# One convolution filter's rows, transposed on VectorE inside partition quadrants and loaded in four parts

## The chip, the core and the metric

The kernel runs on one core of one Trainium2 chip. The metric is the device time of one execution, in microseconds (us). Engines are named as the profile names them: PE (TensorE's matmuls), PEld (its weight loads), DVE (VectorE), ACT (ScalarE), POOL (GpSimd) and SP (SyncE, whose queue issues most of the DMAs). L278 is line 278 of the kernel before.

## What is computed

All inputs are bf16. `x` is [2048, 512] (tokens by channels); the filter `ssm_k` is [512, 2048] (channels by taps), so it takes 2 MB.

```python
kv = shift(k) * v            # shift: four taps per channel, along the tokens
y  = irfft(rfft(kv_padded) * rfft(ssm_k_padded))[:2048]   # a causal convolution per channel, 2048 long
y  = y + kv * ssm_D          # one factor per channel
h  = x + layernorm(x) * y
out = h + relu(layernorm(h) @ w1) @ w2      # w1 [512, 1376], w2 [1376, 512]
```

## The kernel before

The convolution is done in the frequency domain, with a Fourier transform cut into two stages of small matmuls; all tables of sines are made on the chip. The order of the work on each engine is written out by hand (`tc.manual_schedule()`), so each engine executes its instructions in the order in which the code issues them. Four PSUM buffers of two banks each (`bank2`) go round in turn.

**The front of the kernel**, which the change is about, makes two things: the filter's first-stage spectrum, and `kv`.

- *Loads* (L123 to L137, all on SP's queue). The four shift taps; then `ssm_k` in one DMA of 2 MB (L124), where partition p gets the four channels p, 128+p, 256+p and 384+p, a row of 4 KB each; then eight transposing DMAs: of `k` and `v` in four pieces of 512 tokens each (k0, v0, k1, v1, ... here), which put channels on partitions and tokens along the row. `ssm_D` comes over ACT's queue.
- *Fills* (L158): 22 matmuls on zeros, whose result nobody reads.
- *Tables.* POOL makes index ramps and two unit matrices (L162 to L184), a mask `dmask` that carries `ssm_D` in 16 copies (L236) and products of indices (L238). DVE makes the first-stage matrices `f1hi` and `f1lo` (L210 to L215), the product `tsn` (L222) and reductions of it and of `r2` (`wrap13`, L220). ACT takes the sines (L147, L226, L262) and makes the 16 diagonal matrices of the shift taps (L204).
- *The filter's rows* (`to_rows`, L271 to L284, called at L312). Two bf16 values make one 32-bit word. 32 PE transposes of 128 by 128 words put time groups on the partitions and channels along the row; ACT and DVE copy them from PSUM to `kfl` (L281, L283).
- *Stage one* (`stage1`, L286 to L309): for each group `gb` of 0 to 7, 32 small matmuls (L294), then two sums with `dmask` on DVE (L306) and two casts on ACT (L309). Groups 0 and 1 read channels 0 to 31 of each row of `kfl`, 2 and 3 the next 32, and so on.
- *Taps* (`taps`, L329 to L337): for each piece c and half h, eight matmuls with the diagonals give the shifted `k` in PSUM, and DVE multiplies it by `v` in place (L337). This needs k's piece c on PE, v's on DVE.

The loop at L343 goes through groups 0 to 6, with one `taps` behind each of the first six, and sines and index work between; `taps(3, 0)` and `taps(3, 1)` stand ahead of group 6. Behind the loop POOL makes tables (L360 to L385), the transposes of `kv` (L391, `to_rows` again) wait for the last product of the taps, group 7 follows, and the rest of the kernel (spectrum of `kv`, products, inverse transform, the two layer norms and the two matmuls with `w1` and `w2`) follows in PE's order. The results leave in 17 stores (L679) on ACT's queue. Their target's address pattern is 4 blocks of 32 rows:

```python
dst = bass.AP(tensor=out_d.tensor, offset=out_d.offset + t * D + d0, ap=[[16 * D, 4], [64 * D, 32], [1, w]])
nc.scalar.dma_start(out=dst, in_=o[:, d0:d0 + w])
```

Of the kernel before, what the change touches and what calls it, by code (L numbers as in the profile page):

```python
# [9 lines left out]
ALU = mybir.AluOpType  # L10
BF16 = mybir.dt.bfloat16
F32 = mybir.dt.float32
# [3 lines left out]
P = 128  # L16
# [40 lines left out]
def kernel(  # L57
# [13 lines left out]
    nc = tc.nc  # L71
# [5 lines left out]
    DC = D // P  # L77
# [13 lines left out]
    early = pl.push("early", side="right")  # L91
# [5 lines left out]
    BK = bkp.tile([P, 2, 32, 32, DC * 2], F32R, tag="K", name="BK")  # L97
# [21 lines left out]
    r2 = G[:, 0:2048].rearrange("p (a b) -> p a b", a=32)  # L119
# [1 line left out]

    wsh = consts.tile([P, DC, KS], BF16, name="wsh")
    nc.sync.dma_start(out=wsh[:], in_=A_shift_k.rearrange("(r p) j -> p r j", p=P))  # L123
    nc.sync.dma_start(out=sk, in_=A_ssm_k.rearrange("(c p) t -> p c t", p=P))  # L124
    draw = small([DC * P], BF16)
    for dp in range(2):
        src = bass.AP(tensor=A_ssm_D.tensor, offset=A_ssm_D.offset, ap=[[0, 1], [1, DC * P]])
# [1 line left out]
    zero = consts.tile([P, P], BF16, name="zero")  # L129
    nc.vector.memset(zero[:], 0.0)  # L130
    nc.vector.memset(kT[0][:, :, 0:16], 0.0)
    for c in range(4):
        if c == 0:
            nc.sync.dma_start_transpose(out=kT[c][:, :, 16:CH + 16], in_=k_d[0:CH, :])
        else:
            nc.sync.dma_start_transpose(out=kT[c], in_=k_d[CH * c - 16:CH * c + CH, :])
        nc.sync.dma_start_transpose(out=vT[:, :, CH * c:CH * c + CH], in_=v_d[CH * c:CH * c + CH, :])  # L137

    TURN = 2.0 * math.pi * SIN_SHRINK
    nbias = consts.tile([P, 1], F32, name="nbias")  # L140
# [16 lines left out]

    fill(bank2("psz")[:, 0, :], 22)  # L158

    n1i = early.tile([P, 1], I32, name="n1i")  # L160
    for s in range(0, P, 32):
# [6 lines left out]
    r3 = small([64], I32)  # L168
# [4 lines left out]
        nc.gpsimd.memset(f[:], 0.0)  # L173
    ident = early.tile([P, P], BF16, name="ident")
    identw = early.tile([P, P], F32, name="identw")
    for t in (identw, ident):
        nc.gpsimd.memset(t[:], 0.0)
        nc.gpsimd.affine_select(out=t[:], in_=t[:], compare_op=ALU.not_equal, fill=1.0,
                                base=0, pattern=[[-1, P]], channel_multiplier=1)
    nc.gpsimd.iota(r2, pattern=[[2, 32], [128, 64]], base=1, channel_multiplier=0)  # L180
    pi4 = consts.tile([P, 2], I32, name="pi4")
    nc.gpsimd.iota(pi4[:], pattern=[[0, 2]], base=0, channel_multiplier=1)
# [10 lines left out]
    _turns(nc, t1[:, 0:32], r1[:], n1c[:], 128, True)  # L193
    _turns(nc, t1[:, 32:64], r1[:], n1c[:], 128, False)
    t3 = small([2, 64], I32)
    _turns(nc, t3[:, 0, :], r3[:], n2c[:], 64, True)
    _turns(nc, t3[:, 1, :], r3[:], n2c[:], 64, False)
    f1f = small([64], F32)
    f1d = small([64], F32)
    _sin(f1f[:, 0:32], t1[:, 0:32], 128)  # L200
    _sin(f1f[:, 32:64], t1[:, 32:64], 128, neg=True)
    for rg in range(DC):
        for j in range(KS):
            nc.scalar.mul(out=wdiag[:, rg, j, :], in_=ident[:], mul=wf[:, rg, j:j + 1])  # L204
    dsc = small([2, 64], F32)
    dpm = small([2, 64], F32)
    _sin(dsc[:], t3[:], 64)

    f1h = small([64], BF16)
    nc.vector.tensor_copy(out=f1h, in_=f1f)  # L210
# [7 lines left out]
    def wrap13(t):  # L218

        nc.vector.tensor_scalar(out=t, in0=t, scalar1=19, scalar2=19, op0=ALU.logical_shift_left, op1=ALU.arith_shift_right)  # L220

    nc.vector.tensor_single_scalar(out=tsn, in_=r2, scalar=n2c[:], op=ALU.mult)  # L222
    wrap13(tsn)

    def big_sin(out, turns, scale):
        nc.scalar.activation(out=out, in_=turns, func=ACT.Sin, scale=scale * TURN / 8192)  # L226

    dmask = early.tile([P, 2, 2, 16, 2, DC], BF16, name="dmask")
    nc.gpsimd.memset(dmask[:], 0.0)
    for dp in range(2):  # L230
        row = slice(64 * dp, 64 * dp + 1)
        for rp in range(2):
            for sp in range(2):
                src = draw[row, 256 * rp:256 * rp + 256].rearrange("p (r u s l d) -> p r u s l d", r=2, s=2, l=2, d=2)[:, :, :, sp, :, dp]
                for w in range(2):
                    nc.gpsimd.tensor_copy(out=dmask[row, rp, sp, :, w].rearrange("p u (r l) -> p r u l", l=2), in_=src)  # L236

    nc.gpsimd.tensor_scalar(out=r2, in0=r2, scalar1=n2c[:], scalar2=2048.0, op0=ALU.mult, op1=ALU.add)  # L238

# [9 lines left out]
    def ec_turns(q):  # L249
        w = ecw[q]  # L250
        nc.gpsimd.iota(w[:, 1, :].rearrange("p (i a n) -> p i a n", i=4, a=4), pattern=[[1, 4], [16, 4], [64, 32]],
                       base=4 * q, channel_multiplier=0)
        for h, off in ((0, 4096 + 2048), (1, 0)):
            nc.gpsimd.tensor_scalar(out=w[:, h, :], in0=w[:, 1, :], scalar1=k1o[:], scalar2=float(off),
                                    op0=ALU.mult, op1=ALU.add)

    def ec_wrap(q):
        nc.vector.tensor_single_scalar(out=ecw[q], in_=ecw[q], scalar=8191, op=ALU.bitwise_and)
# [12 lines left out]
    def to_rows(src, h, fl):  # L271

        srcw = src.bitcast(F32).rearrange("p c (a w) -> p (c a) w", w=32)
        o = fl.bitcast(I32)
        for eng, i0, n in {1: (("D", 0, 8),), 3: (("A", 0, 4), ("D", 4, 4))}.get(h, (("A", 0, 8),)):
            pst = bank2("pst").rearrange("p b (i c) -> p (b i) c", i=4)[:, 0:n]
            for i in range(n):
                nc.tensor.transpose(out=pst[:, i, :], in_=srcw[:, :, 8 * h + i0 + i], identity=identw[:])  # L278
            oi = o[:, :, 8 * h + i0:8 * h + i0 + n]
            if eng == "A":  # L280
                nc.scalar.copy(out=oi.bitcast(F32), in_=pst.rearrange("p i c -> p c i"))  # L281
            else:
                nc.vector.tensor_single_scalar(out=oi, in_=pst.bitcast(I32).rearrange("p i c -> p c i"),  # L283
                                               scalar=0, op=ALU.bitwise_or)  # L284
# [23 lines left out]
                                    .to_broadcast([P, 8, 16, 4]), op=ALU.add)  # L308
            nc.scalar.copy(out=o[1 - rp][:, 1], in_=pv[1 - rp][:, 1])  # L309

    for h in range(4):
        to_rows(sk, h, kfl)  # L312
    wrap13(r2)
    for t, sh, op in ((0, 2, ALU.logical_shift_right), (1, 3, ALU.bitwise_and)):
        nc.vector.tensor_single_scalar(out=pi4[:, t:t + 1], in_=pi4[:, t:t + 1], scalar=sh, op=op)
    nc.vector.tensor_scalar(out=k1o[:], in0=pi4[:, 0:1], scalar1=2.0, scalar2=1.0, op0=ALU.mult, op1=ALU.add)
    nc.vector.tensor_copy(out=rof[:], in_=pi4[:, 1:2])
    for t, v in ((esc, TURN / 8192), (ebi, -0.5 * TURN)):
        nc.vector.tensor_scalar(out=t[:], in0=rows4[:], scalar1=rof[:], scalar2=v, op0=ALU.is_equal, op1=ALU.mult)
    big_sin(st[:, :, 0:64], tsn, 1)  # L320

    def more_sines(i):
        half = slice(16 * (i % 2), 16 * (i % 2) + 16)
        if i < 2:
            big_sin(st[:, half, 128:192], tsn[:, half], -1)
        else:
            big_sin(st[:, half, 64:128], r2[:, half], 1)

    def taps(c, h, each=2):  # L329
        ps = bank2("pkv")  # L330
        for i in range(2):
            for j in range(KS):
                nc.tensor.matmul(out=ps[:, i, :], lhsT=wdiag[:, 2 * h + i, j, :],  # L333
                                 rhs=kT[c][:, 2 * h + i, 16 - j:CH + 16 - j], start=(j == 0), stop=(j == KS - 1))
# [5 lines left out]
    inv3 = consts.tile([P, 2, 2, 64], F32R, name="inv3")  # L340
    inv12 = consts.tile([P, 2, 64], F32R, name="inv12")
    ones = consts.tile([P, P], F32R, name="ones")
    for gb in range(7):  # L343
        if gb == 6:
            taps(3, 0)
            taps(3, 1, 1)
            ec_sins(0, (2, 3))
        stage1(kfl, BK, gb, dmask)
        if gb < 4:
            more_sines(gb)  # L350
        if gb == 1:
            ec_turns(0)
        if gb == 3:
            ec_wrap(0)
        if gb in (4, 5):
            ec_sins(0, (gb - 4,))
        if gb < 6:
            taps(gb // 2, gb % 2)

    nc.gpsimd.memset(inv3[:].bitcast(F32), 0.0)  # L360
    nc.gpsimd.tensor_tensor(out=dpm[:, 0, :], in0=dsc[:, 0, :], in1=dsc[:, 1, :], op=ALU.add)
# [396 lines left out]
```

## Time and profile before

| | |
|---|---|
| median of 3 runs | 210.63 us (210.59 to 212.22) |
| the profiled execution's own time | 210.65 us |
| its span, first to last instruction | 208.9 us |
| busy: PE, DVE, ACT, POOL | 197.8, 141.3, 116.8, 70.0 us |
| `ssm_k` issued, landed | 1.25, 9.33 us |
| first stage-one matmul | 14.40 us |
| first transpose of `kv` | 36.47 us |

In rows of the chain and the timeline the first number is the start in us from the span's beginning, the second the duration; `out<-in` are the program's tiles (E holds `ssm_k`, `kfl`, v and k's first two pieces; F holds k's last two), xN how many instructions the row merges. "SPq" and "ACTq" are the queues that issue DMAs: such a row's duration is that of issuing, not of the transfer. In rows of windows the columns are: window, its length, busy time of PE, PEld, DVE, ACT and POOL (each with the count of instructions), granted TensorE clock, mean busy share of the core's 16 DMA engines, GB/s.

### The profile page before, as it was taken

The page shows a single profiled execution, that of the slowest core. Times are in us where ns is not written, and L with a number is a line of the kernel's source. Part 1 is how long each engine was busy: PE and PEld are TensorE (multiplying, and loading weights), DVE is VectorE, ACT ScalarE, POOL GpSimd, SP SyncE. Part 2 cuts the span into 40 slices and gives each one's busy share as a digit, 9 for nine tenths or more (in the row PEclk, how much of TensorE's full clock was granted, in tenths as well). Part 3 has the DMA queues.
Part 4 walks back from the last instruction along what each step waited for, and adds up shares of the span by engine and source line. Part 5 has one row for each costly group of instructions (what it writes and reads, how often), then busy time and mean ns, then how long its engine had stood idle before and what let it go on. Part 6 is the DMA issues. An engine that isn't in the chain of part 4 may idle for free.

```text
span 208.9 us, 4331 instructions
## 1 busy us (share of the span) xinstructions
PE 197.8 (95%) x1735; PEld 137.5 (66%) x1735; DVE 141.3 (68%) x244; ACT 116.8 (56%) x188; POOL 70.0 (33%) x118
## 2 busy tenths in 40 slices
PE   8689999988999999999999999999999999999991
PEld 3375554977899999799998944457444844444450
DVE  5978997699588989997743676987088742261131
ACT  5788777688677778677692059302960065026300
POOL 7964603980366599231003030722002100002000
PEclk9999999999999999999999999999999999999999
DMA  5999970000700000038415999999806705110011
GB/s 151 352 212 189 194 126 2 3 5 4 269 3 0 3 0 3 0 100 104 88 26 161 223 210 210 173 161 119 114 12 127 142 24 100 30 54 20 0 50 50
DMA packets 47819, 19.91 MB, mean 95 GB/s; under 512 B 42711, under 2 KB 46265, under 8 KB 47801
## 3 DMA queue, kind: packets, MB, share of 16 engines
q1 hardware_dynamic: 44144, 16.15, 41.2%
q10 hardware_dynamic: 3656, 3.51, 6.0%
q8 instruction: 13, 0.21, 0.4%
q14 instruction: 6, 0.04, 0.1%
HBM read 7.02 MB, written 2.10 MB: 44 GB/s over the span
## 4 chain that ended last, share of the span: by engine, by line
PE 83%; DVE 5%; ACT 5%; DMA 4%; issue 1%; SPq 0%; DVEq 0%; ACTq 0%
PE ps2m L674 18%; PE ps1m L658 14%; PE psi L553 11%; PE u L431 8%; PE us L441 8%; PE ps L294 8%; PE pkv L333 7%; PE pz L646 5%; DMA E<-in_A_ssm_k_dram 4%; PE pst L278 3%; ACT BX L262 2%; DVE st L511 1%; ACT M L660 1%; DVE qT L632 1%; DVE BK L448 1%
## 5 line engine op out<-in xcount | busy, mean ns | idle before, releaser
L660 ACT ACTIVATE M<-ps1m 128x512 bf16<-128x512 f32 (+1 forms) x44 | 25.0, 601 | 50.0 <-PE ps1m L658 39.6
L674 PE MATMUL ps2m<-M 128*128 128x512 bf16 (+3 forms) x187 | 38.8, 367 | 0.0
L674 PEld LDWEIGHTS <-M 128*128 128x128 bf16 (+1 forms) x187 | 18.2, 98 | 20.1 <-ACT M L660 0.4
L658 PEld LDWEIGHTS <-w 128*128 128x128 bf16 (+1 forms) x176 | 17.4, 100 | 20.4 <-issue 0.7
L381 POOL TENSOR_TENSOR smc<-st 64x256 fp32r<-64x256 f32 x32 | 22.8, 731 | 15.8 <-PE us L441 15.0
L515 POOL TENSOR_SCALAR rstd<-mv 128x4 f32<-128x4 f32 x8 | 2.2, 276 | 70.4 <-DVE mv L513 70.4
L676 DVE SCALAR_TENSOR_TENSOR M<-ps2m,rstd,M 128x512 bf16<-128x512 f32 (+1 forms) x13 | 9.2, 707 | 24.0 <-PE ps2m L674 15.5
L448 DVE TENSOR_TENSOR BK<-u,ktu 128x512 fp32r<-128x512 f32 x32 | 20.6, 685 | 4.9 <-PE us L441 2.7
L553 PE MATMUL psi<-inv,BX 128*128 128x256 f32 x64 | 21.5, 341 | 0.2
L553 PE MATMUL psi<-inv,BK 128*128 128x128 f32 x128 | 21.6, 254 | 0.0
L421 ACT COPY ktu<-u 128x512 f32<-128x512 f32 x32 | 18.0, 588 | 5.2 <-DVE BK L448 2.4
L553 PEld LDWEIGHTS psi<-inv,BK 128*128 128x128 f32 x128 | 20.1, 197 | 0.0
L658 PE MATMUL ps1m<-xT,w 128*128 128x512 bf16 (+1 forms) x88 | 19.6, 379 | 0.2 <-ACT M L660 0.2
L658 PE MATMUL ps1m<-M,w 128*128 128x512 bf16 (+1 forms) x88 | 19.3, 380 | 0.0
L431 PE MATMUL u<-BK,st 64*128 64x256 f32 x128 | 14.2, 303 | 0.1
L431 PE MATMUL u<-BX,st 64*128 64x256 f32 x128 | 13.0, 284 | 0.0
L553 PEld LDWEIGHTS psi<-inv,BX 128*128 128x128 f32 x64 | 12.4, 197 | 0.7 <-DVE BK L448 0.7
L309 ACT CAST BK<-ps 128x512 fp32r<-128x512 f32 x16 | 9.4, 585 | 6.2 <-PE ps L294 4.0
L511 DVE BATCH_NORM_STATS2 st<-M 128x6 f32<-128x512 bf16 x20 | 12.3, 676 | 0.0
L632 DVE TENSOR_TENSOR qT<-pz,qT 128x2048 bf16<-128x2048 f32 x2 | 4.6, 2292 | 10.9 <-DMA qT<-M 6.8
L337 DVE TENSOR_TENSOR E<-pkv,E 128x1024 bf16<-128x1024 f32 (+1 forms) x9 | 9.9, 1104 | 2.7 <-PE pkv L333 2.7
L441 PE MATMUL us<-BK,smc 128*128 128x256 f32 x64 | 10.8, 294 | 0.7 <-ACT BX L267 0.6
(126 smaller groups left out, 403.5 us busy)
## 6 DMA issues: line engine op xcount, KB each, us to landing
E<-in_A_ssm_k_dram SPq DMA_DIRECT2D x1, 2048.0 KB
out_dram<-M ACTq DMA_DIRECT2D x15, 128.0 KB
w<-in_B_w_dram SPq DMA_DIRECT2D x1, 1376.0 KB
M<-in_B_w_dram ACTq DMA_DIRECT2D x1, 1280.0 KB
M<-in_A_q_dram SPq DMA_DIRECT2D x8, 128.0 KB
xh<-in_A_q_dram SPq DMA_DIRECT2D x4, 128.0 KB
xr<-in_A_q_dram SPq DMA_DIRECT2D x4, 128.0 KB
out_dram<-M ACTq DMA_DIRECT2D x2, 64.0 KB
```

Of the source, the lines that this page charges most:

```text
L294: nc.tensor.matmul(out=pss[rp][:, gi // 2, :, gi % 2, :], lhsT=fl[rows, 2 * g:2 * g + 2, :].rearrange("p d n -> p (d n)"), rhs=f[rows].rea ...
L333: nc.tensor.matmul(out=ps[:, i, :], lhsT=wdiag[:, 2 * h + i, j, :], rhs=kT[c][:, 2 * h + i, 16 - j:CH + 16 - j], start=(j == 0), stop=(j = ...
L381: nc.gpsimd.tensor_tensor(out=smc[pq, c % 3, i, :, 64 * dp:64 * dp + 64], in0=st[pq, ks, 64:128].bitcast(F32), in1=st[pq, ks, 0:64].bitcas ...
L421: nc.scalar.copy(out=kt[:], in_=ps)
L431: nc.tensor.matmul(out=ps[:, dp, 256 * x:256 * x + 256], lhsT=t[pq], rhs=cols((BK, BX)[x], pq, k1, i), start=(i == 0), stop=(i == 1), tile ...
L441: nc.tensor.matmul(out=ps[:, k % 2, 256 * x:256 * x + 256], lhsT=smc[:, k // 4 % 3, i, k % 4, :], rhs=cols((BK, BX)[x], slice(0, P), k, i) ...
L448: nc.vector.tensor_tensor(out=o, in0=ps[:, :, 256:512].rearrange("p b (g x) -> p b g x", x=8), in1=kt[:].rearrange("p b (g x) -> p b g x", ...
L511: nc.vector.bn_stats(out=st[:, i, :], in_=src[:, i, :])
L553: nc.tensor.matmul(out=o if part == 0 else o[:, P * part - P:P * part], lhsT=src[:, g // 2, :, g % 2::2].rearrange("p c r -> p (c r)"), rh ...
L658: nc.tensor.matmul(out=ps1[:fsz, :].rearrange("p (i t) -> p i t", i=4), lhsT=w1[:, c, fc * P:fc * P + fsz], rhs=hT[sc][:, :, c, :], start= ...
L660: nc.scalar.activation(out=h1T[:fsz, fc, :], in_=ps1[:fsz, :], func=ACT.Relu)
L674: nc.tensor.matmul(out=ps2, lhsT=h1T[:ksz, fc, i * P:(i + 1) * P], rhs=w2[:ksz, fc, d0:d0 + w], start=(fc == 0), stop=(fc == NFC - 1))
```

## The change

`ssm_k` is loaded in four parts of 512 KB, each with 32 channels of each of the four partition quadrants, two of them ahead of k0 and v0 and two behind. The rows come from four DVE instructions that transpose 32 by 32 blocks of words (`transpose_part`), from SBUF to SBUF, in place of the 32 PE transposes and their copies from PSUM. The fills go from 22 to 18. On POOL `dmask` is made ahead of the second unit matrix and the ramp `r2`, and POOL makes the product `tsn`, which was DVE's. On DVE the small `pi4` and `rows4` instructions stand ahead of the transposes; `wrap13` of `tsn` and `r2` and the turns `t3` move behind, among the groups. On ACT the last four diagonals, and the sines, move too. The groups and taps go in another order: groups 0 to 3, `taps(0, 0)`, `taps(0, 1)`, 4, 5, `taps(1, 0)`, 6, and then the other five taps.

```diff
-    nc.sync.dma_start(out=sk, in_=A_ssm_k.rearrange("(c p) t -> p c t", p=P))
...
+    def load_part(c):
+        nc.sync.dma_start(out=sk[:, c, :], in_=A_ssm_k.rearrange("(r c m) t -> c r m t", r=DC, c=DC)[c])
...
+    load_part(0)
+    load_part(1)
+    load_kv(0)
+    load_part(2)
+    load_part(3)
+    for c in range(1, 4):
+        load_kv(c)
...
-    fill(bank2("psz")[:, 0, :], 22)
+    fill(bank2("psz")[:, 0, :], 18)
...
+    unit_matrix(ident)
+    dmask = early.tile([P, 2, 2, 16, 2, DC], BF16, name="dmask")
+    nc.gpsimd.memset(dmask[:], 0.0)
...
+                    nc.gpsimd.tensor_copy(out=dmask[row, rp, sp, :, w].rearrange("p u (r l) -> p r u l", l=2), in_=src)
+
+    unit_matrix(identw)
     nc.gpsimd.iota(r2, pattern=[[2, 32], [128, 64]], base=1, channel_multiplier=0)
...
-    _turns(nc, t3[:, 0, :], r3[:], n2c[:], 64, True)
-    _turns(nc, t3[:, 1, :], r3[:], n2c[:], 64, False)
...
-    for rg in range(DC):
+    def diagonals(rg):
         for j in range(KS):
             nc.scalar.mul(out=wdiag[:, rg, j, :], in_=ident[:], mul=wf[:, rg, j:j + 1])
+
+    for rg in range(3):
+        diagonals(rg)
...
-    nc.vector.tensor_single_scalar(out=tsn, in_=r2, scalar=n2c[:], op=ALU.mult)
-    wrap13(tsn)
+    nc.gpsimd.tensor_scalar(out=tsn, in0=r2, scalar1=n2c[:], scalar2=0.0, op0=ALU.mult, op1=ALU.add)
...
-    for h in range(4):
-        to_rows(sk, h, kfl)
-    wrap13(r2)
     for t, sh, op in ((0, 2, ALU.logical_shift_right), (1, 3, ALU.bitwise_and)):
         nc.vector.tensor_single_scalar(out=pi4[:, t:t + 1], in_=pi4[:, t:t + 1], scalar=sh, op=op)
...
-    big_sin(st[:, :, 0:64], tsn, 1)
+
+    def transpose_part(c):
+
+        nc.vector.transpose(out=kfl.bitcast(F32)[:, 32 * c:32 * c + 32, :].rearrange("p m w -> p w m"),
+                            in_=sk.bitcast(F32)[:, c, :].rearrange("p (n w) -> p w n", w=32))
...
-    for gb in range(7):
-        if gb == 6:
-            taps(3, 0)
-            taps(3, 1, 1)
-            ec_sins(0, (2, 3))
-        stage1(kfl, BK, gb, dmask)
...
-        if gb < 6:
-            taps(gb // 2, gb % 2)
+    def spectrum(*gbs):
+        for gb in gbs:
+            stage1(kfl, BK, gb, dmask)
+
+    transpose_part(0)
+    transpose_part(1)
+    spectrum(0, 1)
+    diagonals(3)
+    spectrum(2, 3)
+    taps(0, 0)
+    transpose_part(2)
+    wrap13(tsn)
+    taps(0, 1)
+    big_sin(st[:, :, 0:64], tsn, 1)
+    spectrum(4)
+    transpose_part(3)
+    more_sines(0)
+    spectrum(5)
+    more_sines(1)
+    ec_turns(0)
+    _turns(nc, t3[:, 0, :], r3[:], n2c[:], 64, True)
+    _turns(nc, t3[:, 1, :], r3[:], n2c[:], 64, False)
+    _sin(dsc[:], t3[:], 64)
+    taps(1, 0)
+    wrap13(r2)
+    spectrum(6)
+    more_sines(2)
+    taps(1, 1)
+    more_sines(3)
+    ec_wrap(0)
+    for c, h in ((2, 0), (2, 1), (3, 0)):
+        taps(c, h)
+        ec_sins(0, (2 * (c - 2) + h,))
+    taps(3, 1, 1)
+    ec_sins(0, (3,))
```

As the DMAs stand in the built program, a part's load has the target pattern [128 partitions, 1, 2048 elements] and the source pattern [4 blocks, 32 rows, 2048 elements]; the single load before has 128 as the outermost size on both sides.

More of the change, by code (lines that the diff above doesn't have):

```diff
@@ L131, with load_kv @@
     nc.vector.memset(kT[0][:, :, 0:16], 0.0)
-    for c in range(4):
+    def load_part(c):
+        nc.sync.dma_start(out=sk[:, c, :], in_=A_ssm_k.rearrange("(r c m) t -> c r m t", r=DC, c=DC)[c])
+    def load_kv(c):
         if c == 0:
@@ L175, with unit_matrix @@
     identw = early.tile([P, P], F32, name="identw")
-    for t in (identw, ident):
+    def unit_matrix(t):
         nc.gpsimd.memset(t[:], 0.0)
@@ L179 @@
                                 base=0, pattern=[[-1, P]], channel_multiplier=1)
+    unit_matrix(ident)
+    dmask = early.tile([P, 2, 2, 16, 2, DC], BF16, name="dmask")
+    nc.gpsimd.memset(dmask[:], 0.0)
+    for dp in range(2):
+        row = slice(64 * dp, 64 * dp + 1)
+        for rp in range(2):
+            for sp in range(2):
+                src = draw[row, 256 * rp:256 * rp + 256].rearrange("p (r u s l d) -> p r u s l d", r=2, s=2, l=2, d=2)[:, :, :, sp, :, dp]
+                for w in range(2):
+                    nc.gpsimd.tensor_copy(out=dmask[row, rp, sp, :, w].rearrange("p u (r l) -> p r u l", l=2), in_=src)
+    unit_matrix(identw)
     nc.gpsimd.iota(r2, pattern=[[2, 32], [128, 64]], base=1, channel_multiplier=0)
@@ L201 @@
     _sin(f1f[:, 32:64], t1[:, 32:64], 128, neg=True)
-    for rg in range(DC):
+    def diagonals(rg):
         for j in range(KS):
             nc.scalar.mul(out=wdiag[:, rg, j, :], in_=ident[:], mul=wf[:, rg, j:j + 1])
+    for rg in range(3):
+        diagonals(rg)
     dsc = small([2, 64], F32)
     dpm = small([2, 64], F32)
-    _sin(dsc[:], t3[:], 64)
     f1h = small([64], BF16)
@@ L220, in wrap13 @@
         nc.vector.tensor_scalar(out=t, in0=t, scalar1=19, scalar2=19, op0=ALU.logical_shift_left, op1=ALU.arith_shift_right)
-    nc.vector.tensor_single_scalar(out=tsn, in_=r2, scalar=n2c[:], op=ALU.mult)
-    wrap13(tsn)
+    nc.gpsimd.tensor_scalar(out=tsn, in0=r2, scalar1=n2c[:], scalar2=0.0, op0=ALU.mult, op1=ALU.add)
     def big_sin(out, turns, scale):
         nc.scalar.activation(out=out, in_=turns, func=ACT.Sin, scale=scale * TURN / 8192)
[L228 to L236, printed above, removed]
     nc.gpsimd.tensor_scalar(out=r2, in0=r2, scalar1=n2c[:], scalar2=2048.0, op0=ALU.mult, op1=ALU.add)
@@ L342 @@
     ones = consts.tile([P, P], F32R, name="ones")
-    for gb in range(7):
-        if gb == 6:
-            taps(3, 0)
-            taps(3, 1, 1)
-            ec_sins(0, (2, 3))
-        stage1(kfl, BK, gb, dmask)
[L349 to L356, printed above, removed]
-        if gb < 6:
-            taps(gb // 2, gb % 2)
+    def spectrum(*gbs):
[32 more added lines that the diff above has]
+    ec_sins(0, (3,))
     nc.gpsimd.memset(inv3[:].bitcast(F32), 0.0)
```

## The prediction

> **What bounds the kernel now.** I read the whole chain of waits first: nearly all of it is PE.
>
> ```profile
> PE 83%; DVE 5%; ACT 5%; DMA 4%; issue 1%; SPq 0%; DVEq 0%; ACTq 0%
> ```
>
> So a change at the front pays only if it lets PE's long stretch begin, or end, earlier. The same chain in order of time, for the front:
>
> ```profile
> 1.25 8.08 DMA E<-in_A_ssm_k_dram
> 9.46 4.07 PE pst L278 x32
> 13.56 0.70 DVE E L283
> 14.40 1.07 PE ps L294 x32
> ...
> 29.75 5.30 PE pkv L333 x24
> 35.05 1.04 PE ps L294 x32
> 36.09 0.38 issue
> 36.47 2.94 PE pst L278 x24
> ```
>
> `ssm_k` lands at 9.33, its transposes and their last copy hold PE until 14.40, and then PE works without a gap until 36.09. At 36.47 the transposes of `kv` begin; they need the last product of the taps. I take 36.47 as the mark: the code behind it is the same in both kernels, so a shift of the mark is a shift of the end. Next the loads, in the timeline of SP's queue:
>
> ```profile
> 1.25 0.49 SPq L124 DMA_DIRECT2D E<-in_A_ssm_k_dram  x1
> 1.79 7.29 SPq L134 DMA_TRANSPOSE E<-in_A_k_dram  x1
> 9.13 2.18 SPq L137 DMA_TRANSPOSE E<-in_A_v_dram  x1
> ...
> 25.25 2.95 SPq L137 DMA_TRANSPOSE E<-in_A_v_dram  x1
> ```
>
> The queue works in order: k0 could not be handed over while `ssm_k` was moving (7.29 us, until 9.08), and the last piece, v3, is issued until 28.20. The windows tell how fast it goes:
>
> ```profile
> core 0: us, PE busy (x) PEld busy (x) DVE busy (x) ACT busy (x) POOL busy (x), PEclk, DMA share, GB/s
> 4.00:8.50 4.50, 3.56 (x16) 1.36 (x14) 4.33 (x15) 4.50 (x17) 4.33 (x16) 1.00 1.00 407
> 9.50:30.00 20.50, 19.62 (x266) 12.85 (x267) 17.60 (x28) 15.22 (x20) 10.07 (x22) 1.00 1.14 197
> 30.00:31.00 1.00, 1.00 (x7) 0.41 (x6) 1.00 (x3) 0.76 (x2) 0.00 (x0) 1.00 0.00 0
> 200.00:201.00 1.00, 1.00 (x7) 0.43 (x5) 0.39 (x1) 0.00 (x0) 0.00 (x0) 1.00 0.27 95
> 205.50:207.00 1.50, 0.00 (x0) 0.00 (x0) 0.00 (x0) 0.00 (x0) 0.00 (x0) 1.00 0.28 86
> ```
>
> The reader is to see three things. The whole `ssm_k` load uses all 16 DMA engines: share 1.00, 407 GB/s, so 25.4 GB/s each. The transposing loads never rest long and end at 30.0, shortly before PE asks for them. And a store, even with several queued, keeps the share at 0.27, which is 4 of 16 engines, at 86 to 95 GB/s. A store's target pattern is [4 blocks, 32 rows, ...] against 128 partitions; each new part of `ssm_k` has this very form on its source side.
>
> Last, the POOL and DVE rows that the moved work is priced by:
>
> ```profile
> 5.47 0.13 POOL L182 IOTA pi<- 128x2 int32 x1
> 6.53 5.15 POOL L236 COPY dmask<-E 1x64 bf16<-1x64 bf16 x16
> 8.23 1.33 DVE L222 TENSOR_SCALAR G<-G,n2c 128x2048 int32<-128x2048 int32 x1
> 11.53 1.23 DVE L283 TENSOR_SCALAR E<-pst 128x1024 int32<-128x1024 int32 x1 [0.70 <-PE pst L278]
> 15.73 0.23 DVE L319 TENSOR_SCALAR esc<-rows,rof 128x4 f32<-128x4 f32 x1
> 25.45 0.69 DVE L258 TENSOR_SCALAR G<-G 128x1024 int32<-128x1024 int32 x1
> ```
>
> **The change, part by part.**
>
> *The load in four parts.* This is the step that I think decides. I take it that a part runs on 4 DMA engines, as the stores do. `ssm_k` is 2.097 MB. On 16 engines it takes 2.097 / 407 = 5.15 us at full rate; on 4 at 25.4 GB/s each, 101.7 GB/s, all four parts take 20.6. The queue in front of the last transposing loads grows by 20.6 - 5.15 = 15.45 us: 5.15 ahead of k0 and v0 (two parts take 10.3, against 5.15 for the whole), and 10.3 between v0 and k1, for the other two. Seen from one of the four engines it is the same: 128 rows of 4 KB instead of 32. All transposing loads need those engines too, so the other twelve running ahead does not help them. The first two parts are in at about 9.3 and 14.5, k0 and v0 come 5.15 later than before, the other two parts at 24.2 and 29.4, and k1 to v3 come 15.45 later. Bounds from rows: at the stores' 86 GB/s the parts take 24.4 (shift 19.2); at 16 engines the shift is nothing but four issues of some 0.5 instead of one.
>
> The Trainium skill, page "DMA: Bandwidth & Descriptors", section "Why a DMA increments its semaphore by 16 and not by 1", has a rule that speaks against this change: a DMA from this kind of queue gets the largest number of engines up to 16 that divides the outermost size of both patterns. By it a part with 4 on the source side and 128 on the target gets 4, and the sum stays as above. The stores' 0.27 agrees, with the 4 on their target side; if the target alone decided, the part would get 16 and the sum would be that of the second case below.
>
> *What PE then waits for.* The order of PE ends with `taps(2, 0)` to `taps(3, 1)`. k3 is in at about 28.5 before: SP hands over v3 until 28.20, and the queue's pause from 27.5 to 28.5 (34 GB/s) ends there, with v3's traffic behind it. PE starts `taps(3, 0)` at 29.68 + 1.79 = 31.47, a third into the row of 24 matmuls, 5.37 us long; so k3 had 3.0 us to spare. After: 28.5 + 15.45 = 43.95. Two taps take 3.58, until 47.53. From the end of the taps on PE (35.05) to the mark (36.47) it was 1.42: two products on DVE. The mark falls at 48.95, against 36.47: **+12.5 us**.
>
> *What is taken off the front.* The transposes (4.07), the copy behind them (0.70) and four fills (4 x 0.215) leave PE's chain, some 4.9 us, and group 6 (1.04) no longer stands behind `taps(3, 1)`. None of it is worth anything while k3 comes at 44: all of PE's work from the first group on, 21.7 us, has room before.
>
> *The word transposes.* No row shows one. Bounds for 1024 words: 0.69 (L258, SBUF to SBUF) and twice 1.23 (L283, which wrote the same tile in the same stride). I take 1.23, the row of the same size and target. The first two run in idle time, once part 0 is in. The third and fourth make DVE wait for parts, at 24.2 and 29.4. Queued behind the third are `wrap13(tsn)`, the product of `taps(0, 1)` and group 4's sums, so ACT's sines and POOL's index work wait too; behind the fourth are group 5's sums, the turns and the product of `taps(1, 0)`, which waits for v1 (about 35) anyway. From there to 43.95 DVE has two products, one reduction, two sums, an index reduction and two more products, some 8 us at 1.23 and below; even at twice 1.23 the fourth ends at 31.9. Cost nothing; the late loads are the cover, and without it two of them would stand in DVE's stage (second case).
>
> *POOL and DVE ahead of the first transpose.* The `pi4` and `rows4` instructions now stand ahead of it on DVE, and their inputs behind `dmask`, the unit matrix and `r2` on POOL. The copies took 5.15, but two of them (1.24 and 1.32) ran beside DVE's L222 and L220, and the others start 0.175 apart; with these gone 16 take 2.8, from 3.6 to 6.4, the unit matrix 0.55, `r2` 1.9, so `rows4` is ready at about 9.4 and DVE's six small instructions (0.79) end near 10. Part 0 is there at 9.3, so this costs 0.7 at most, under cover. POOL's product of `tsn` (2.0, as L238) and ACT's four late diagonals (4 x 0.3) lie in the same waiting time.
>
> *What is late next.* ACT's last sines end near 46, POOL's clearing and tables take 2.8 and 8.9 from there, until 57.7; PE wants them at 52.25 + 12.5 = 64.7. Covered. The load of `w1` waits for the same products as before and moves with the mark.
>
> *The clock.* Of the fills before, the first nine start 0.43 apart and the rest 0.215, while the granted clock reads 1.00 throughout: PE begins at half pace. After the change PE has several pauses of 3 us and more. Before `taps(3, 0)` the pause is from about 41 to 44. If PE fell back there, two taps would take 3.6 more; I leave that to the range. The page "TensorE: Matmul & The Clock Gate", "Part 1: The HAM clock gate", puts the fall at an idle window of about 3.4 us, which 3 us would not fill; by it the sum stays, and no row here shows a fall after such a pause (1.9 us at 7.55 is the longest in the front).
>
> *Sum.* 210.65 (the profiled execution, 1.75 of it around its span; the median is 210.63) + 12.5 = **223.2 us**.
>
> **The rivals.**
>
> *Second case: the parts run on 16 engines.* Then part 0 is in by about 5.5 and DVE becomes the bound. Its first transpose starts at 10.0, its second ends at 12.4. From 16.00 (its first sum before) to 36.37 (its last product) DVE was busy 17.6 of 20.4. Added to that: two transposes 2.46, two reductions 2.45, the turns 0.9, group 6's sums 1.28: 24.7, so its last product ends at 37.1 without any idle time and at 39.9 with all of that of before, against 36.37; halfway, 38.5, is 2.1 later: 212.8 us (211.4 to 214.2). For it: no load before has a 4 on its source side alone. Against it: the stores.
>
> *Third case, the other side: no slower.* 16 engines, and a transpose at 0.69 (L258) instead of 1.23. Four of them save 4 x 0.54 = 2.2 against the second case, which is all that it loses: 210.6 us (209.2 to 212.0). It decides from a transpose of about 0.7 on, and needs the first condition too.
>
> *Fourth: four engines, but the pauses in the transposing loads vanish.* Before, they show 10, 18 and 34 GB/s in the windows 18 to 19, 24 to 25 and 27.5 to 28.5, some 2.6 us without traffic. If they do not come back, and the slow start of the first load (up to 1.3) is shorter, the shift is 8.6: 219.2. This is within the range of the first case.
>
> **How the numbers follow.** Four engines: 0.86; second case 0.09; third 0.05. The first case runs from 217.0 (fourth case, with another 2 us because the four engines, left alone, may move a transposing load faster) to 228.5 (half of the stores' slower rate, +1.9, and a half-pace PE, +3.6). That leaves out the other cases and some 0.04 of this one, under 0.2, so it is my range. Faster than 208.5: 0.02, for what the third case leaves open below its range. Within 1%, which is about what a measurement of this kernel can tell from no change: 0.09, half of the second case and the rest of the third. Slower: 0.89.
>
> **What would show it.** Right: a DMA share near 0.25 and some 100 GB/s while a part moves; parts about 5 us apart; DVE's third and fourth transpose waiting for a DMA; PE waiting for k3 until about 44; the mark near 49. Wrong: a share near 1 with parts 1.3 us apart (second case: DVE busy without gaps from 12 on); a transpose far over 2.5; or the mark early while something behind it is late.

## The result, and the profile after

The changed kernel takes 223.94 us (median of 4 runs, 223.74 to 226.33) against 211.35 for the kernel before beside it (4 runs, 210.59 to 212.22): ratio 1.062 [1.053, 1.071], slower. The forecast was 223.2, in a range of 217.0 to 228.5. The four runs before fall in two pairs, near 210.6 and 212.1; beside the experiments below, with 7 to 13 runs, their median is 210.56 to 210.77. The profiled execution took 223.97 us, its span 221.7; before it was 210.65 and 208.9.

The page's shares of the chain come first. PE held 83% of it before; now a sixth is SP's queue.

```profile
PE 68%; SPq 17%; ACT 4%; DVE 4%; DMA 2%; issue 2%; DVEq 0%; ACTq 0%
```

The same chain in order of time, from the first load to the first transposes of `kv` (the mark, L291 now):

```profile
2.59 12.62 SPq L137
...
15.26 2.36 SPq L140
...
18.84 12.56 SPq L139
...
31.44 2.22 SPq L140
...
33.71 3.31 SPq L139
...
39.11 5.26 DMA F<-in_A_k_dram
44.37 0.05 issue
44.42 3.65 PE pkv L347 x16
48.06 1.64 issue
49.71 2.94 PE pst L291 x24
```

No compute engine stands in it before 44.42. L137 is k0, L139 a later piece of k, L140 a piece of v. Twice the queue is held for 12.6 us over a single piece of k: each time two parts are still moving. Then k3 lands at 44.37, two taps take 3.65, the last products on DVE follow, and the mark is at 49.71 instead of 36.47. For the 1.64 us ahead of the mark the chain names no cause ("issue"); the timeline has DVE there, held by the last piece, v3:

```profile
47.05 2.42 DVE L351 TENSOR_TENSOR E<-pkv,E 128x1024 bf16<-128x1024 f32 x3 [1.66 <-DMA E<-in_A_v_dram]
```

The product of `taps(3, 0)` could have started near 46.2, when its taps were done, and waited for v3 until 47.05; the three products end at 49.47. With k3 alone the last two would have followed the taps' end (48.06) and taken 1.29, until about 49.4. So k3 and v3, neighbours in the queue, bind almost together; v3 adds some 0.1.

How fast a part moves is in the windows: 6 to 14 lies in the first pair of parts, 24 to 30 in the second, 213 to 214 in a store.

```profile
6.00:14.00 8.00, 0.67 (x7) 0.18 (x7) 4.78 (x10) 2.02 (x7) 7.49 (x13) 0.81 0.26 104
24.00:30.00 6.00, 3.12 (x37) 1.97 (x36) 4.68 (x4) 0.33 (x1) 0.00 (x0) 0.83 0.25 102
213.00:214.00 1.00, 1.00 (x6) 0.49 (x5) 0.55 (x1) 0.00 (x0) 0.00 (x0) 1.00 0.27 94
```

The last two columns answer to the 1.00 and 407 GB/s of before: a share of a quarter, 102 to 104 GB/s; the store shows 0.27 and 94. (The share counts a packet whole in the window in which it starts, so it can pass 1.) The timeline of DVE shows when parts come, and two durations that the prediction had smaller:

```profile
9.44 0.21 DVE L325 TENSOR_SCALAR pi<-pi 128x1 int32<-128x1 int32 x2 [2.94 <-POOL pi L206]
...
9.95 1.78 DVE L329 TENSOR_SCALAR esc<-rows,rof 128x4 f32<-128x4 f32 x1
...
11.77 2.07 DVE L333 STREAM_TRANSPOSE E<-E 128x1024 f32<-128x1024 f32 x1
15.50 2.07 DVE L333 STREAM_TRANSPOSE E<-E 128x1024 f32<-128x1024 f32 x1 [1.66 <-DMA E<-in_A_ssm_k_dram]
...
26.55 2.02 DVE L333 STREAM_TRANSPOSE E<-E 128x1024 f32<-128x1024 f32 x1 [1.28 <-DMA E<-in_A_ssm_k_dram]
...
32.70 2.08 DVE L333 STREAM_TRANSPOSE E<-E 128x1024 f32<-128x1024 f32 x1
```

The second and third transposes wait for their parts, until 15.50 and 26.55. A transpose takes 2.07 us, and `esc`, four elements a row, takes 1.78 where it took 0.23 before.

### The profile page after: what moved, and what is told of

Same layout as the page of the kernel before. It is cut to its first block, busy times and chain, and to the rows that moved or that the text cites. A ratio compares the mean times of both kernels' runs of the same rounds, so it can differ in the third digit from the quotient of the medians.

```text
span 221.7 us, 4259 instructions
## 1 busy us (share of the span) xinstructions
PE 198.2 (89%) x1699; PEld 137.4 (62%) x1699; DVE 146.2 (66%) x245; ACT 113.8 (51%) x185; POOL 71.4 (32%) x119
## 4 chain that ended last, share of the span: by engine, by line
PE 68%; SPq 17%; ACT 4%; DVE 4%; DMA 2%; issue 2%; DVEq 0%; ACTq 0%
PE ps2m L707 17%; PE ps1m L691 13%; PE psi L586 10%; PE u L464 8%; PE us L474 7%; SPq L139 7%; SPq L137 6%; PE pz L679 5%; PE ps L307 4%; SPq L140 3%; DMA F<-in_A_k_dram 2%; PE pkv L347 2%; ACT BX L275 2%; PE pst L291 1%; DVE st L544 1%
## 5 line engine op out<-in xcount | busy, mean ns | idle before, releaser
L707 PEld LDWEIGHTS <-M 128*128 128x128 bf16 (+1 forms) x187 | 18.2, 98 | 20.0 <-ACT M L693 0.4
L307 PE MATMUL ps<-f_hi,E 64*128 64x128 bf16 x128 | 11.9, 268 | 11.9 <-DVE E L333 10.2
L307 PEld LDWEIGHTS <-E 64*128 64x128 bf16 x256 | 10.8, 122 | 14.6 <-DVE E L333 11.6
L322 ACT CAST BK<-ps 128x512 fp32r<-128x512 f32 x16 | 8.9, 585 | 14.9 <-PE ps L307 10.2
L347 PEld LDWEIGHTS <-E 128*128 128x128 bf16 x64 | 6.3, 103 | 11.0 <-issue 2.7
```

The lines of the kernel that those rows point to most:

```text
L307: nc.tensor.matmul(out=pss[rp][:, gi // 2, :, gi % 2, :], lhsT=fl[rows, 2 * g:2 * g + 2, :].rearrange("p d n -> p (d n)"), rhs=f[rows].rea ...
L707: nc.tensor.matmul(out=ps2, lhsT=h1T[:ksz, fc, i * P:(i + 1) * P], rhs=w2[:ksz, fc, d0:d0 + w], start=(fc == 0), stop=(fc == NFC - 1))
```

## The experiments

In the table, "engines" is the DMA share times 16 while the filter moves (full when it is near 1), "first transpose" the start of DVE's first one in the timeline. In the lines of the edits, the kernel named is the base. All ratios are against the kernel before, whose median was 210.56 to 210.77 beside these runs.

| kernel | base | engines | first transpose | mark | us | ratio |
|---|---|---|---|---|---|---|
| a3_before_one_block | before | 16 | none | 36.45 | 210.61 | 0.9997 [0.9978, 1.0016] |
| a2_before_8_blocks | before | 8 | none | 44.44 | 218.78 | 1.0385 [1.0364, 1.0406] |
| a2_before_4_blocks | before | 4 | none | 55.10 | 229.33 | 1.0886 [1.0864, 1.0908] |
| a5_after_rows_of_128 | after | 16 | 11.72 | 44.91 | 219.12 | 1.0389 [1.0356, 1.0422] |
| a1_quadrant_loads | after | 16 at half rate | 11.74 | 44.77 | 218.96 | 1.0392 [1.0375, 1.0409] |
| c1_all_parts_ahead | after | 4 | 11.75 | 54.15 | 228.40 | 1.0821 [1.078, 1.0863] |
| b2_small_behind_own_load | after | 4 | 10.14 | 50.16 | 224.19 | 1.0628 [1.059, 1.0666] |
| b1_small_ones_behind | a5 | 16 | 6.13 | 39.62 | 213.74 | 1.0127 [1.0086, 1.0167] |
| b4_quadrants_small_behind | a1 | 16 at half rate | 8.11 | 41.31 | 216.05 | 1.026 [1.0213, 1.0308] |
| b3_small_behind_contiguous | b1 | 16 | 6.12 | 36.64 | 211.35 | 1.002 [0.9996, 1.0043] |
| d1_before_word_transposes | before | 16 | 10.77 | 42.98 | 217.46 | 1.03 [1.0248, 1.0353] |

**Theory:** a part whose source pattern begins with 4 blocks moves on 4 engines, and the queue then brings k3 late. **Rivals:** loading in parts costs by itself; the parts' place among k and v costs; DVE's late and long work sets the end, and DMA only looks guilty.

### The number of blocks, alone

Three kernels leave all of the kernel before as it is but for the load, which comes in four DMAs, all ahead of k0. They differ in how many blocks of rows a DMA's source has.

```diff
-    nc.sync.dma_start(out=sk, in_=A_ssm_k.rearrange("(c p) t -> p c t", p=P))
+    for c in range(DC):
+        nc.sync.dma_start(out=sk[:, c, :], in_=A_ssm_k[c * P:(c + 1) * P, :])                                    # a3
+        nc.sync.dma_start(out=sk[:, c, :], in_=A_ssm_k.rearrange("(r c m) t -> c r m t", r=8, c=DC)[c])   # a2, r=8 or 4
```

> The kernel before, with its 2 MB load of ssm_k cut into four loads of 512 KB of 128 consecutive rows each, all ahead of k0 (outermost size 128 on both sides). Both theories give nearly no change, since each load can use all 16 DMA engines: share near 1.0, some 400 GB/s, the last part landed at 9.3 to 10.5, time 210.3 to 212.0 us. If cutting the load in four were itself the cost, the parts would be about 5 us apart and the time 225 or more.

> The same with 8 blocks of 16 rows in each load (again a permuted filter, same work). If the number of blocks sets the number of engines, share 0.5, about 203 GB/s, parts 2.6 us apart, the last landed at about 15.5: 216 to 220 us. If 4 blocks are slow for another reason (the distance of the rows in memory, or any pattern that is not one block), this is as slow as with 4 blocks, 227 us or more.

> The kernel before, with the same four loads of 512 KB ahead of k0, but each of 4 blocks of 32 rows, the pattern that the change introduced. It permutes the filter's channels, so it computes with a permuted filter; the work is the same. Theory (4 blocks on one side put a load on 4 engines): share 0.25 and about 102 GB/s, parts 5.1 us apart, the last landed at about 25.7 (first part 10.4 as in the profile after, plus 3 x 5.1); the transposes start 16.4 us later, and PE has gone to half pace in the wait, which costs 1 to 3 more: 227 to 230 us. Rival (the time went to the order of the queue, not to the pattern): as the run with one block, 210.3 to 212 us.

A window inside the filter's load, of each in this order:

```profile
4.00:8.00 4.00, 3.61 (x16) 1.40 (x14) 3.87 (x12) 2.41 (x9) 3.87 (x13) 1.00 1.02 381
```

```profile
9.00:15.00 6.00, 0.00 (x0) 0.00 (x0) 1.82 (x2) 0.00 (x0) 4.64 (x7) 0.77 0.52 187
```

```profile
16.00:24.00 8.00, 0.00 (x0) 0.00 (x0) 0.00 (x0) 0.00 (x0) 0.00 (x0) 0.50 0.26 103
```

Shares of 1.02, 0.52 and 0.26, at 381, 187 and 103 GB/s: share and rate follow the number of blocks. Four DMAs instead of one cost nothing: 210.61. Both other kernels wait for the filter itself, as the chain of the one with 4 blocks shows:

```profile
3.16 22.55 DMA E<-in_A_ssm_k_dram
25.71 0.14 issue
25.85 6.31 PE pst L279 x32
```

The 32 transposes on PE, 4.07 before, take 6.31, because PE stood still for so long that its clock fell; that is why this kernel loses 18.6 us where the filter comes 25.71 - 9.33 = 16.4 later. The rule quoted in the prediction from the Trainium skill ("DMA: Bandwidth & Descriptors", "Why a DMA increments its semaphore by 16 and not by 1") stands for the source side too: 4, 8 and 128 as the source's outermost size gave a quarter, a half and all of the rate.

### The same cause in the changed kernel

`a5` keeps the parts' places in the queue and changes only their source; `a1` keeps the rows as they are and loads each pair of parts in four DMAs, one for each quadrant.

```diff
-        nc.sync.dma_start(out=sk[:, c, :], in_=A_ssm_k.rearrange("(r c m) t -> c r m t", r=DC, c=DC)[c])
+        nc.sync.dma_start(out=sk[:, c, :], in_=A_ssm_k[P * c:P * c + P, :])                                      # a5
+        for r in range(DC):                                                                                      # a1
+            rows = A_ssm_k[128 * r + 32 * c:128 * r + 32 * c + 64, :]
+            nc.sync.dma_start(out=sk[32 * r:32 * r + 32, c:c + 2, :], in_=rows.rearrange("(c m) t -> m c t", c=2))
```

> The changed kernel with one thing undone: each part reads 128 consecutive rows in place of four blocks of 32, in the same place in the queue (so the filter's channels come in another order: the part of the computation that is changed). If the four-block source is what puts the load on 4 of 16 DMA engines and that holds back k3, the parts take about 1.3 us each at about 380 GB/s, k3 is in by about 31, and the time is that of the quadrant loads, 217.5 to 219.5; what is left over the kernel before is then VectorE's and has nothing to do with DMA. If the parts' place in the queue (two of them behind k0 and v0, each change between plain and transposing transfers paid for once more) is what costs, the time stays at 222 or above.

> The changed kernel, with each two of its parts brought by four loads, one for a partition quadrant (32 partitions by 2 rows of 4 KB, outermost size 32 on both sides), at the same places in the queue: the same bytes to the same addresses. Theory (engines): share near 1.0, 1 MB in by about 7, k3 by about 30, and DVE becomes the bound. DVE's first transpose starts at 11.8 as in the profile after, the second ends at 15.9; from there it has 17.65 (busy before from 16.0 to 36.4) + 2 x 2.07 (transposes) + 2.45 (reductions) + 0.9 (turns) + 1.28 (group 6) = 26.4, so its last product ends at 42.3 or later against 36.4: 216 to 219 us. Rival (two parts between v0 and k1, and k0 behind two parts, delay the transposing loads by their place): k3 at 40 or later, 222 to 225 us.

219.12 and 218.96: some 4.9 us come back, no more. No DMA stands in either chain. That of `a5` has POOL, DVE and then PE at the front:

```profile
3.64 1.57 POOL dmask L201 x8
...
7.38 1.89 POOL G L204
...
9.90 1.78 DVE esc L329
11.68 0.12 DVE ebi L329
11.80 2.02 DVE E L333
13.82 0.05 issue
13.87 3.64 PE ps L307 x44
```

The last piece of its queue, v3, stands in the timeline of SP as

```profile
25.40 2.40 SPq L140 DMA_TRANSPOSE E<-in_A_v_dram  x1
```

It is handed over by 27.80, where the kernel before was done at 28.20 and the changed kernel at 44.25. So the place of the parts is not what costs, and the four engines are not all that costs: with them gone a second bound lies 8.4 us above the kernel before (44.91 - 36.47).

### All parts ahead

```diff
     load_part(0)
     load_part(1)
-    load_kv(0)
     load_part(2)
     load_part(3)
-    for c in range(1, 4):
+    for c in range(4):
         load_kv(c)
```

> The changed kernel with all four parts ahead of k0 in SyncE's queue, none behind k0 and v0. It computes the whole reference. Engines: four parts of 5.15 us stand ahead of k3 either way, so k3 still comes at about 44 and the time is 223 to 226 (k0 and v0 come near 30, so TensorE has more left to do after they come, which may add up to 2 us). Rival, that going back and forth between the two kinds of transfer costs by itself: two changes fewer, 1 to 3 us gained, 221 to 223.

228.40, more than either view expected, and the mark 4.4 later than in the changed kernel. The queue was done with v3 1.6 us sooner (issued until 42.63 instead of 44.25), which may be what two changes fewer between the kinds of transfer are worth; but k3 does not stand in the chain:

```profile
6.39 22.11 DMA E<-in_A_k_dram
...
28.55 0.61 PE pkv L344
...
32.18 1.23 DVE E L348
33.40 1.95 DVE E L330
...
39.57 2.02 DVE E L330
```

k0 lands at 28.50. DVE's third transpose (33.40) is issued behind the product of `taps(0, 0)`, so it waits for k0 although its part came long before; groups 4 and 5 wait for it in turn. The order of DVE was written for two parts ahead of k0 and two behind, and with the slow parts that split is worth 4.4 us. I had put the late k0 at up to 2.

### The second bound: DVE's start, and the transposes

`b1` takes `a5` and moves the six instructions on `pi4` and `rows4` behind the product of `taps(0, 0)`; `b2` makes the same move with the changed kernel's own load; `b3` takes `b1` and lets the transposes read and write contiguously.

```diff
-    for t, sh, op in ((0, 2, ALU.logical_shift_right), (1, 3, ALU.bitwise_and)):
...
     taps(0, 0)
+    for t, sh, op in ((0, 2, ALU.logical_shift_right), (1, 3, ALU.bitwise_and)):
...
-        nc.vector.transpose(out=kfl.bitcast(F32)[:, 32 * c:32 * c + 32, :].rearrange("p m w -> p w m"),
-                            in_=sk.bitcast(F32)[:, c, :].rearrange("p (n w) -> p w n", w=32))
+        nc.vector.transpose(out=kfl.bitcast(F32)[:, 32 * c:32 * c + 32, :].rearrange("p m w -> p (m w)"),
+                            in_=sk.bitcast(F32)[:, c, :])
```

> The kernel with one-block parts, and on DVE the six small instructions on pi4 and rows4 moved from ahead of the first transpose to behind the product of taps(0, 0). If it is their wait for POOL that holds the first transposes, the first starts at about 6.6 (part 0 in, the first-stage matrices done) instead of 11.8, PE pauses 2 us instead of 7 before the first group and doesn't lose its clock there (group 0 and 1 took 3.5 us together, 2.1 before): some 4.5 to 6 us earlier, 212 to 215 us. If DVE is the bound by its work alone from the first group on, the same gain, since it starts earlier. If the later waits (order of groups, taps and transposes) set the end, less than 2 us: 216 or more.

> The changed kernel with its own four-block load, and only the six small VectorE instructions on pi4 and rows4 moved behind the product of taps(0,0). It computes the whole reference. With a load of 128 rows a part the same move was worth 5.2 us. Here k3 comes at 44 whatever VectorE does, so the theory that k3 sets the end of this stage expects nothing: 223.2 to 224.4, the first transpose of kv at 49 to 50 as in the changed kernel. The rival, that VectorE's late start is itself part of the 13 us, expects 219 to 222.

> The kernel with parts of 128 rows and the six small instructions moved back (213.74 us), whose four transposes now read and write contiguously (the filter's words come in another order: the part of the computation that is changed). If the 32-word step is what doubles a transpose, each takes 1.1 to 1.25 us instead of 2.07, and as the first transpose and the third stand in the chain, 1.5 to 3 us are gained: 210.8 to 212.3, which is about the kernel before's. If the order of the work is what is left of the difference, 213 to 214.

With full-rate parts the move is worth 219.12 - 213.74 = 5.4 us, since the first transpose starts at 6.13 instead of 11.72. With the slow parts it is worth nothing: 224.19. What comes free at the front is not paid for while the queue sets the end. The first lines here are `b1`'s, of its first transpose and its `esc`; the second fence has the four transposes of `b3`, with shortest, median and longest in ns:

```profile
6.13 2.09 DVE E L327
...
8.26 1.11 PE ps L307 x32
...
18.24 0.23 DVE esc L366
```

```profile
L327 DVE STREAM_TRANSPOSE E<-E x4: 1201/1236/1245, 6.1 to 22.6; 128x1024 f32<-128x1024 f32 x4
```

`esc` is back at 0.23: POOL runs no product beside it now. And without the step of 32 words a transpose takes 1.24 us; the kernel is then level with the kernel before, 211.35. From `b1` to `b3` the mark moves by 2.98: the two long transposes in `b1`'s chain give 2 x 0.82; the rest, 1.3, I put down to PE, which no longer falls to half its clock (mean 1.00 in this execution), but that was not tried by itself. Which of the two steps costs was looked at in one more kernel (with the parts of `a5`, each transpose in another form):

> The kernel with one-block parts, its four transposes each with another access pattern on 1024 words (what they write is not the filter's rows in the order wanted; the later work is the same): the first reads and writes consecutive words, the second reads consecutive words and writes with a step of 32 words, the third reads with the step and writes consecutively, the fourth takes 2048 bf16 values, consecutive on both sides. If the step costs the time, the first takes 1.1 to 1.3 us and one or both of the next 2.07. If the word size does, the first three all take 2.0 to 2.1 and the fourth, with twice as many values of half the size, about the same 2.1 to 2.3.

It took 218.51 us in one run. Contiguous on both sides a transpose took 1.23 us, with the step only on the write 1.91, only on the read 1.91, and as 2048 bf16 elements, contiguous, 2.30. The first line has the first three (shortest, median and longest in ns):

```profile
L342 DVE STREAM_TRANSPOSE E<-E x3: 1231/1914/1914, 11.7 to 23.2; 128x1024 f32<-128x1024 f32 x3
...
29.29 2.30 DVE L336 STREAM_TRANSPOSE E<-E 128x2048 bf16<-128x2048 bf16 x1
```

So one step, on either side, already costs nearly what both do (2.0 to 2.1). The change needs the one on the read, since it must bring words that lie 32 apart into one block; a form at 1.24 us would make another transform of it, and none was tried.

### The word transposes, alone

The kernel before, with only PE's transposes and their copies replaced by the four on DVE (its one load brings whole quadrants):

```diff
-    for h in range(4):
-        to_rows(sk, h, kfl)
+    for c in range(4):
+        nc.vector.transpose(out=kfl.bitcast(F32)[:, 32 * c:32 * c + 32, :].rearrange("p m w -> p w m"),
+                            in_=sk.bitcast(F32)[:, c, :].rearrange("p (n w) -> p w n", w=32))
```

> The kernel before with its one load, and only the four DVE transposes in place of the PE transposes and their copies (on the rows as that load places them, so the filter's channels are permuted; same work). PE's 4.07 and the copy's 0.70 go, DVE gets 4 x 2.07 = 8.3 and loses 1.92. They stand behind the reduction of tsn, so 10.8 to 19.1; the reduction of r2 and the small instructions end at 21, the first sums start there instead of at 16.0, PE has group 0 from 13 on. DVE's 2.75 us without work from 16.0 to 36.4 take up some of the 5: 3 to 5 us slower, 213.5 to 216 us. If the PE transposes were the costlier way here, it would be 210 or less.

217.46, 1.5 us above the range expected. Two lines of its chain:

```profile
10.85 7.79 DVE E L312 x4
18.64 1.08 DVE G L220
```

The four transposes end at 18.64, where the last copy from PSUM ended at 14.26 before: 4.4 us of the mark's 6.5. While they run PE has little to do (1.51 of the 3.4 us up to 19.2), and its clock is at half from 19.2 to 26.05. In the chain that stretch holds one group (1.86, where a group took 1.00 to 1.10 before) and one `taps` (3.08 for 1.84), which is the other 2.1. Taking work off PE made PE slower here.

### The best form found

`a1`'s loads with `b1`'s move: nothing of the computation is left out or put in another order.

> The best form of this change that the earlier runs point to, and it computes the whole reference: parts loaded in pairs, by four loads of 32 partitions each (all 16 DMA engines, at 200 GB/s), and the six small VectorE instructions behind the product of taps(0,0). With parts of 128 rows the same move brought 219.12 to 213.74. Here the first pair is in at about 7.5 instead of 6.1 for the first part, so up to 1.4 us may be lost again: 213.5 to 215.5, still slower than the kernel before, by the step of 32 words in the transposes and by the order of the work. If instead the quadrant loads hold the transposing loads back once VectorE no longer does, 217 or above.

216.05, half a us above the range expected: the first pair is in at 8.0, not 7.5. It is 7.9 us better than the changed kernel and still 1.026 [1.0213, 1.0308] of the kernel before. None of the forms tried that computes the reference beats the kernel before.

## Why the prediction was right, and where it was not

- **The load in four parts** (right in cause and rate, too small in time): 0.25 to 0.26 and 102 to 104 GB/s, for 101.7 predicted. But the parts came later than worked out: the first by 10.14 in `b2`, whose DVE waits for it, the second and third by 15.50 and 26.55, for 9.3, 14.5 and 24.2. The sum gave the first pair the start of the whole load before, and the second pair none; the windows show 23 GB/s from 2.6 to 4.0 (before, 174 from 2.4 to 4.0) and 27 from 19 to 20. Each pair held the queue about 1 us longer than worked out, so the hand-over of k1 ended at 31.40 against 13.95, 17.45 later and not 15.45.
- **What PE waits for** (right, the number in part by luck): k3 at 44.37 for 43.95, two taps 3.65 for 3.58, from there to the mark 1.64 for 1.42. From the hand-over of k1 to the landing of k3 the transposing loads took 12.97 us for some 14.55 before, and this 1.6 made up for most of the 2.0 by which the parts were late. The sum also had no term for v3, which came within 0.1 us of setting the end itself. The mark is 49.71 for 48.95, +13.2 for +12.5. The span grew by 12.8, and what lies around it by 0.5 (from 1.75 to 2.27), which the sum had left alone; with it the time is 223.97.
- **The front's 4.9 us worth nothing** (right): `b2` shows it, with the first transpose 1.6 us earlier and no gain. (The three terms named add up to 5.6; PE's fills end at 7.55, ahead of the filter, and are no part of the chain.)
- **The word transposes** (wrong in size, no cost here): 2.07 for 1.23. The row that I took, L283, wrote in the same step but read from PSUM; neither bounding row was a transpose. The upper bound, 2.46, holds it. The cover that was named, the late loads, did hide it. Of the two waits for a part, the third transpose had its own (1.28 us); the fourth found its part there.
- **POOL and DVE ahead of the first transpose** (wrong in size, no cost here): "0.7 at most" was 1.6 (the first transpose at 11.77, and at 10.14, when its part is in, in `b2`), as `esc` ran into POOL's product of `tsn`, which this change had moved to POOL. POOL's product runs from 9.74 to 11.71, and `esc` ends with it:

```profile
9.74 1.97 POOL L246 TENSOR_SCALAR G<-G,n2c 128x2048 int32<-128x2048 int32 x1
```

  The kernel before had shown this already: a DVE instruction of 64 elements a row beside POOL's ramp `r2` took 1.98, the next of the same form 0.25.

```profile
3.57 1.94 POOL L180 IOTA G<- 128x2048 int32 x1
3.58 1.98 DVE L44 TENSOR_SCALAR E<-E,n2c 128x64 int32<-128x64 int32 x1
...
5.70 0.25 DVE L44 TENSOR_SCALAR E<-E,n2c 128x64 int32<-128x64 int32 x1
```

- **The clock** (wrong): the prediction feared a pause from 41 to 44 ahead of `taps(3, 0)`. There was none: PE had fallen to half its clock earlier, worked until 44, and waited 0.3 us for k3. It had let the Trainium skill's page "TensorE: Matmul & The Clock Gate" ("Part 1: The HAM clock gate") say that 3 us would not be enough to fall. The windows, laid where the clock steps, show otherwise; the first number behind the length is PE's busy time, the third from the end the clock:

```profile
7.50:10.90 3.40, 0.00 (x0) 0.00 (x0) 1.35 (x5) 0.52 (x2) 3.33 (x5) 1.00 0.25 101
10.95:14.30 3.35, 0.41 (x10) 0.41 (x11) 2.89 (x3) 0.00 (x0) 2.73 (x2) 0.50 0.25 102
...
21.30:24.60 3.30, 2.48 (x12) 1.17 (x12) 2.44 (x4) 1.84 (x4) 0.00 (x0) 1.00 3.06 115
24.70:28.00 3.30, 1.04 (x5) 0.29 (x3) 2.02 (x2) 0.00 (x0) 0.00 (x0) 1.00 0.25 103
28.05:31.40 3.35, 2.56 (x45) 2.31 (x47) 3.32 (x4) 1.73 (x1) 0.00 (x0) 0.50 0.27 88
...
34.90:38.20 3.30, 3.30 (x24) 1.45 (x24) 2.48 (x7) 1.83 (x3) 1.86 (x6) 0.50 0.95 212
38.30:41.60 3.30, 3.30 (x32) 1.66 (x29) 3.30 (x5) 1.73 (x3) 3.05 (x7) 1.00 1.20 168
```

  PE was busy for 1.04 of 3.30 us, not idle, and the clock fell for the next three windows. That cost almost nothing only because k3 was later still: PE and k3 arrived within 0.3 us of each other.
- **The second case** (its chance was small, its time wrong): 16 engines give 219.12, not 212.8. Of the 6.3 us between, the long transposes are 2.4 (`b1` against `b3`) and the later start of the first one (11.72 for 10.0) about 1.7, at the 0.96 us per us by which `a5` and `b1` differ. The other 2.2 I can't lay at one door: DVE's busy time was summed as if it ran without new gaps, while from group 4 on DVE, ACT and PE wait for one another in turn, and PE takes groups 0 and 1 at half its clock (3.64 us in the chain of `a5`). So even the third case's condition, 16 engines and a transpose of 0.7, is not to be had here: the contiguous form is 1.24.
- **The fourth case** (pauses in the transposing loads vanish) came in part: behind the last part they moved 210 GB/s (31.40 to 44.37) for 185 (13.95 to 28.50 before), the 1.6 us above. It does not show in the time, since the parts were late by more.

The prediction held because the term that it priced from matching rows, the rate of a pattern with 4 blocks, was also the one that set the end. That it came within 0.8 us is luck in part: two errors of 2.0 and 1.6 us in the queue had opposite signs. The terms priced from rows of another kind were off by half or more, and none of them was on the path.

## What to carry to other kernels

When a load is cut, look at the outermost size of both its patterns, not at its bytes: cut by rows that stay 128 long, four DMAs cost nothing; cut into 4 blocks, the same bytes held the transfers behind them back by some 16 us here. When a bound that a change has brought in is taken away, look for the next before promising the gain: here 4.9 of 13 us came back, and then DVE, which had looked free, was the bound. And work that leaves PE can slow PE, if what remains keeps it too little busy: 1.51 of 3.4 us was too little here, 2.14 was enough.

## What the runs showed of the hardware

- A 32-partition load runs on all engines (share 0.94 to 1.0) and yet moves 200 to 224 GB/s, against 381 for 128 partitions. The Trainium skill, page "SBUF — State Buffer", section "Door 1: The DMA port swizzle (why `[64,N]` ≈ `[32,N]`)", says why: partitions 0 to 31 reach half of the ports; its 189 GB/s is near the rates here.
- DVE's transpose of 1024 words a row takes 1.24 us, and 1.9 to 2.1 with a step of 32 words on the read, the write or both.
- A DVE instruction of four elements took 1.78 us beside a POOL product of 2048, and 0.23 without it; they ended together, at 11.7.
- The granted clock went to 0.50 after stretches of 3.4 us in which PE was busy for 0, 1.04 (both above), 1.12 (`b1`, from 18.2) and 1.51 us (`d1`, from 15.8), and not after 2.14 or 2.48 (from 17.8 and 21.3 in the changed kernel). Where between these the edge lies was not tried. At 0.50 it stayed there through stretches of 2.56 and 2.16 us, and came back after 3.09 and 3.30 (from 28.05, 31.5, 14.4 and 34.9 in the changed kernel).
